# Batch 4's key-value product behind three pieces of group 2's first layer, and the r mix of group 2 ahead of its first square

## The chip, the cores and the metric

The kernel runs on one core of a Trainium2 chip. The metric is the device time of one execution in microseconds (us). The kernel before takes 201.94 us, the median of three runs from 201.52 to 202.92 us.

A core has engines that run beside each other, each with its own in-order queue of instructions: PE (TensorE, matrix products into PSUM), DVE (VectorE, elementwise work), ACT (ScalarE, activations, copies and scalings), POOL (GpSimd, here it only issues the large loads) and SP (SyncE, here it issues stores and small on-chip copies). Engines wait for each other through semaphores. An instruction that waits holds up everything behind it on its engine.

## The reference

Two layers follow each other. The first is a linear attention with an RMS norm per head, over 8 batches, 8 heads, 576 rows and 64 columns:

```
kv  = k^T v                       per batch and head, 64 x 64
out = q kv
out = out / sqrt(mean(out^2) + 1e-6) * g_norm
x   = the heads side by side      8 x 576 x 512
```

The second is a channel mix, in which each row is blended with the row before it of the same batch:

```
xk = mu_k * x + (1 - mu_k) * x_prev
xr = mu_r * x + (1 - mu_r) * x_prev
k  = relu(xk @ w_k)               512 -> 1024
v  = (k * k) @ w_v                1024 -> 512
r  = sigmoid(xr @ w_r)            512 -> 512
result = r * v
```

## The kernel before, in words

The attention goes by batches (0 to 7), each in two halves of four heads (z = 0 and 1). The channel mix goes by nine groups of 512 rows over all batches in one row; group 2 takes rows 1024 to 1535, so it needs the blended rows of batches 1 and 2.

The work is cut into pieces with names, and a hand-written string `ORDER` (L15) lists all of them in one sequence. `emit` (L41) walks through it and gives out the instructions of each piece to its engine. Each engine keeps the sequence in which the string names its own pieces. So moving a name in the string moves that piece in its engine's queue, against the other pieces of that engine alone. Waits are put in automatically, where an instruction reads or overwrites something that another engine handles. `@A` or `@D` behind a name chooses ACT or DVE.

The names that matter here, with B a batch and G a group:

- `ld.kB`, `ld.vB`, `ld.qB` (L226, L221): POOL issues the load of one batch of k, v or q, which is turned into bf16 on the way. The k and v buffers are a ring of three.
- `kvB.01` (L265): PE forms k^T v of batch B in 72 small products of 64x64. It needs that batch's k and v.
- `kcB` (L346, through `copy` at L128) copies the result out of PSUM, `ksB` (L271) sorts its even and odd rows with four products, `kdB` (L350, through `copy`) copies that out.
- `tqB` (L358): DVE transposes q. `uB` (L282): PE forms q kv in 16 products per half of the columns; it needs `kdB` and `tqB`.
- `sqB`, `ssB` (L388), `rsB` (L288): the squares, their sums per head, and one over the root, small and packed. `spB.z` (L430): SP spreads the small result over the partitions by four on-chip copies per half.
- `mulB.z` (L405), `dB.z` (L300), `mkB.z` and `mrB.z` (L136 on DVE, L134 on ACT), `xkB.z` and `xrB.z` (L313): the norm, the difference to the row before, its scaling by mu, and the blended rows for k and for r.
- `kG.F` (L507): four products, an eighth of group G's first layer. Two of them share one PSUM buffer, and then `reluG.H` (L465, ACT, H = F // 2) and `ksqG.H` (L522, DVE) make relu and its square from both.
- `rG.C` (L534) and `sigG.C2` (L544): the r product of 128 rows in four products, and the sigmoid of two of them. `vG.C.P` (L554): four products of the second layer. `outG.C2` (L567) and `stG.C` (L456): the product with the sigmoid on DVE, and the store by SP.

PSUM is a ring of four buffers (`ps`), taken in the order in which the string first uses them; whoever takes one waits until its last reader is done. Batch 2's `xk2.0` and `xk2.1` cover the two halves of the columns that the first layer sums over: of the four products of a piece `k2.F`, the first two read the half z = 0 and the last two read z = 1.

## Time and profile before

| | before |
|---|---|
| median of three runs | 201.94 us |
| the profiled execution, its own time | 201.43 us |
| its span (first to last instruction) | 199.6 us |
| PE busy | 190.3 us (95%) |
| DVE busy | 137.9 us (69%) |
| ACT busy | 122.0 us (61%) |
| POOL busy | 23.6 us (12%) |
| data moved by DMA | 30.63 MB |

The span is what the profile's time axis covers; the execution's own time has 1.83 us around it. The share of PE is an average over the whole span: where PE stands still is seen only in the time order of its instructions. In a timeline row the first number is the start, the second the length, both in us, then the engine, the line, the operation and the tiles (written <- read); the bracket tells how long the engine stood idle before it, and what ended that.

### The profile page before, as it was taken

What the parts mean: (1) busy time and instruction counts of PE and PEld (TensorE: products, weight loads), DVE (VectorE), ACT (ScalarE), POOL (GpSimd) and SP (SyncE); (2) the same over time, 40 slices, a digit from 0 to 9 for tenths busy, and PEclk for the clock granted to TensorE, in tenths of its full rate; (3) what the DMA queues carried; (4) which work ended last, traced back from release to release, by engine and by line L of the source; (5) the groups of instructions that cost most, each with busy time, mean ns of one, the idle gap of its engine ahead of it and who ended that gap; (6) DMA issues with size and microseconds to landing.
All of it is one profiled execution on the core that took longest, in us unless ns stands there. A gap on an engine that the chain in (4) does not pass through costs nothing.

```text
span 199.6 us, 4250 instructions
## 1 busy us (share of the span) xinstructions
PE 190.3 (95%) x1760; PEld 93.1 (47%) x1760; DVE 137.9 (69%) x235; ACT 122.0 (61%) x158; POOL 23.6 (12%) x42
## 2 busy tenths in 40 slices
PE   7899999999998799999999999999999999999992
PEld 2436854454443444444448744444444444444451
DVE  1669988897869396988968598799759421530741
ACT  3365599759967579945868986882319940423420
POOL 7734342041312010000000000000000000000000
PEclk9999999999999999999999999999999999999999
DMA  6999999999999999999402531643203000320344
GB/s 214 211 210 210 203 206 203 215 203 212 216 238 256 218 238 280 251 231 255 172 3 55 152 126 56 192 138 77 44 20 139 0 3 0 124 86 0 145 174 158
DMA packets 21031, 30.63 MB, mean 153 GB/s; under 512 B 1932, under 2 KB 14484, under 8 KB 21012
## 3 DMA queue, kind: packets, MB, share of 16 engines
q0 software_dynamic: 11280, 16.19, 45.3%
q1 hardware_dynamic: 9588, 14.03, 21.9%
q8 instruction: 14, 0.23, 0.4%
q10 hardware_dynamic: 144, 0.13, 0.2%
q14 instruction: 5, 0.04, 0.1%
HBM read 33.56 MB, written 9.44 MB: 215 GB/s over the span
## 4 chain that ended last, share of the span: by engine, by line
PE 76%; DMA 16%; ACT 2%; POOL 2%; issue 1%; DVE 1%; POOLq 0%; ACTq 0%
PE ps L554 28%; PE ps L507 24%; DMA k<-in_k_dram 16%; PE ps L534 13%; PE ps L482 3%; PE ps L265 3%; PE ps L282 2%; ACT relu L465 1%; PE ps L408 1%; PE ps L450 1%; PE ps L388 1%; PE ps L271 1%; POOL v L226 1%; POOL q L221 1%; ACT sq L379 1%
## 5 line engine op out<-in xcount | busy, mean ns | idle before, releaser
L554 PE MATMUL ps<-w_v,sqk 128*128 128x512 bf16 (+1 forms) x296 | 67.2, 374 | 0.0
L507 PE MATMUL ps<-xk,w_k 128*128 128x512 bf16 (+1 forms) x288 | 58.8, 356 | 0.5 <-issue 0.5
L465 ACT ACTIVATE relu<-ps 128x1024 bf16<-128x1024 f32 x36 | 36.5, 1025 | 35.1 <-PE ps L507 31.7
L554 PEld LDWEIGHTS <-sqk 128*128 128x128 bf16 x296 | 27.8, 98 | 32.2 <-issue 2.5
L507 PEld LDWEIGHTS <-w_k 128*128 128x128 bf16 x288 | 27.5, 98 | 26.9 <-issue 1.6
L567 DVE TENSOR_TENSOR out<-ps,sig 128x1024 f32<-128x1024 f32 x16 | 19.4, 1220 | 21.9 <-PE ps L554 12.5
L534 PE MATMUL ps<-w_r,xr 128*128 128x512 bf16 x144 | 34.0, 379 | 0.0
L522 DVE TENSOR_TENSOR sqk<-relu 128x1024 bf16<-128x1024 bf16 x32 | 21.2, 684 | 12.5 <-ACT relu L465 12.2
L544 ACT ACTIVATE sig<-ps 128x1024 bf16<-128x1024 f32 x18 | 18.2, 1024 | 12.4 <-PE ps L534 12.4
L534 PEld LDWEIGHTS <-xr 128*128 128x128 bf16 x144 | 13.8, 98 | 16.3 <-issue 0.5
L379 ACT ACTIVATE sq<-ps 128x576 bf16<-128x576 f32 x32 | 19.9, 652 | 1.8 <-PE ps L282 1.6
L144 ACT ACT_TABLE_LOAD x12 | 15.4, 1283 | 0.9 <-PEq L607 0.7
L358 DVE STREAM_TRANSPOSE qT<-q 128x576 f32<-128x576 f32 (+1 forms) x20 | 14.7, 760 | 1.8 <-DMA q<-in_q_dram 1.6
L136 DVE TENSOR_SCALAR uT<-ps,cols 128x576 bf16<-128x576 f32 x13 | 10.4, 816 | 6.9 <-ACT sq L379 4.8
L136 DVE TENSOR_SCALAR md<-d,cols 128x576 bf16<-128x576 bf16 x44 | 14.0, 370 | 0.4
L134 ACT ACTIVATE uT<-ps,cols 128x576 bf16<-128x576 f32 x15 | 10.9, 742 | 2.9 <-PE ps L282 2.9
L300 DVE TENSOR_TENSOR d<-xT 128x1152 bf16<-128x1152 bf16 (+1 forms) x18 | 12.3, 689 | 0.4
L313 DVE TENSOR_TENSOR xr<-md,xT 128x1152 bf16<-128x1152 bf16 x14 | 10.4, 751 | 1.6 <-ACT md L134 1.4
L405 DVE TENSOR_TENSOR xT<-uT,rs 128x1152 bf16<-128x1152 bf16 x14 | 10.4, 750 | 1.1 <-ACT rs L288 0.6
L313 DVE TENSOR_TENSOR xk<-md,xT 128x1152 bf16<-128x1152 bf16 x14 | 10.4, 754 | 0.6 <-ACT md L134 0.4
L450 PE MATMUL ps<-zero 128*128 128x512 bf16 x30 | 9.4, 454 | 1.2 <-DVE zero L164 1.2
L265 PE MATMUL ps<-v,k 64*64 64x64 bf16 x576 | 7.7, 194 | 2.4 <-DMA k<-in_k_dram 2.1
(53 smaller groups left out, 121.6 us busy)
## 6 DMA issues: line engine op xcount, KB each, us to landing
out_dram<-out SPq DMA_DIRECT2D x35, 256.0 KB, 2.3
v<-in_v_dram POOLq DMA_DIRECT2D x6, 576.0 KB, 22.6
k<-in_k_dram POOLq DMA_DIRECT2D x6, 576.0 KB, 23.1
q<-in_q_dram POOLq DMA_DIRECT2D x6, 576.0 KB, 23.9
rs<-rsc SPq DMA_DIRECT2D x48, 72.0 KB, 3.3
q<-in_q_dram POOLq DMA_DIRECT2D x4, 288.0 KB, 10.0
w_k<-in_moe_w_k_dram POOLq DMA_DIRECT2D x2, 512.0 KB, 11.0
w_v<-in_moe_w_v_dram POOLq DMA_DIRECT2D x2, 512.0 KB, 13.8
```

The costliest lines, as they stand in the source:

```text
L136: nc.vector.tensor_scalar(out=dst, in0=src, scalar1=col, scalar2=None, op0=ALU.mult)
L144: nc.scalar.preload_act_table_set(name)
L313: nc.vector.tensor_tensor(out=dst[:, 2 * z:2 * z + 2, r0:r0 + w], in0=md.t[:, :, cs], in1=xT[:, :, cur], op=ALU.add)
L358: nc.vector.transpose(out=dst[part, js], in_=src[part, js])
L379: sq_ = add("sq" + name, "A", lambda _, ps=ps, sq=sq, cs=cs, w=w: nc.scalar.activation(out=get(sq)[:, :, cs], in_=ps.t[:, :, 0:w], func=AF ...
L465: nc.scalar.activation(out=get(rt), in_=ps.t, func=AF.Relu)
L507: nc.tensor.matmul(get(ps)[:, fc % 2, a0:a1], w_k_sb[:, cc, 128 * fc:128 * fc + 128], xk[:, cc, x0:x0 + a1 - a0], start=(cc == 0), stop=(c ...
L522: nc.vector.tensor_mul(out=get(sqk)[:, 2 * f2:2 * f2 + 2, :], in0=rt.t, in1=rt.t)
L534: nc.tensor.matmul(get(ps)[:, ci % 2, :], xr[:, cc, n0:n0 + 128], w_r_sb[:, cc, :], start=(cc == 0), stop=(cc == NHP - 1))
L544: nc.scalar.activation(out=get(sg), in_=ps.t, func=AF.Sigmoid)
L554: nc.tensor.matmul(get(ps)[:, bank, cs], sqk.t[:, fc, 128 * ci:128 * ci + 128], w_v_sb[:, fc, cs], start=(fc == 0), stop=(fc == NFC - 1))
L567: dv = add(f"out{g}.{c2}", "D", lambda _, ps=ps, sg=sg, ot=ot: nc.vector.tensor_mul(out=get(ot), in0=ps.t, in1=sg.t), deps=ms + [sg_done], ...
```

## The change

Only the string `ORDER` differs, in one stretch. `kv4.01` stood right behind `v1.0.1`, ahead of the spreading of batch 2; it now stands behind `k2.2`, `k2.3` and `k2.0`. `kc4.01` follows it. In the DVE's sequence `ksq2.1` stood ahead of `xr2.0`, `mr2.1` and `xr2.1`; it now stands behind them.

```diff
 ... sq3.01 ss3 v1.0.1
-kv4.01
 sp2.0 sp2.1 rs3 st0.0 mul2.0 d2.0 mk2.0@D xk2.0 mul2.1 d2.1 mk2.1@D
 st0.1 sp3.0 mr2.0@A xk2.1 k2.2 sp3.1 out1.0 k2.3
-kc4.01@A
 out1.1 st1.3 k2.0
+kv4.01 kc4.01@A k2.1
 ks4.01 relu2.1 kd4.01@A st1.0
-ksq2.1 k2.1
-xr2.0 relu2.0 mr2.1@D xr2.1
+xr2.0 mr2.1@D xr2.1 ksq2.1 relu2.0
 tq4.01.0 tq4.01.1 ld.q7.01 k2.4 k2.5 relu2.2 k2.6 r2.2 r2.3 u4.01.0 ...
```

By engine: on PE the sequence was kv4, k2.2, k2.3, k2.0, ks4, k2.1, k2.4 and is now k2.2, k2.3, k2.0, kv4, k2.1, ks4, k2.4. On DVE it was out1.1, ksq2.1, xr2.0, mr2.1, xr2.1, tq4 and is now out1.1, xr2.0, mr2.1, xr2.1, ksq2.1, tq4. The sequences of ACT, POOL and SP are as they were.

More of the change, by code (lines that the diff above doesn't have):

```diff
@@ L15 @@
 ORDER = """
-ldh.k ldh.v seta setp perm ld.q0.0 ld.q0.1 ld.v0.1 ld.k0.1 ld.wk0 ident ld.wk1 ld.v1.1 ld.k1.1 ld.q1.1 ld.wr ld.q1.0 ld.v1.0 ld.k1.0 ld.wv0 ld.wv1 ld.v2.01 ld.k2.01 ld.q2.01 table small zz cst.k0@D cst.k1@A setb cst.v0@A cst.v1@D tq0.0.1 tq0.0.0 z:512 z:512 z:512 z:512 z:512 z:512 z:512 z:512 z:512 z:512 z:512 z:512 z:512 z:512 z:512 z:512 kv0.0 tq0.1.0 kc0.0@A z:512 z:512 ks0.0 tr9 cols kd0.0@A u0.0.0 sq0.00 z:512 z:512 z:512 ss0.00 u0.0.1 rs0.00 mul0.00 d0.00 tq0.1.1 z:512 z:512 kv0.1 ld.k3.01 ld.v3.01 ld.q3.01 sq0.01 kc0.1@A ss0.01 rs0.01 ks0.1 kd0.1@A z:512 z:512 z:512 u0.1.0 sq0.10 xk0.00 z:512 z:512 z:512 ss0.10 mul0.01 d0.01 xk0.01 rs0.10 mul0.10 d0.10 u0.1.1 k0.000 sq0.11 ss0.11 rs0.11 k0.110 xk0.10 k0.100 mul0.11 k0.001 d0.11 xk0.11 relu0.00 xr0.11 xr0.00 k0.010 k0.011 kv1.1 ksq0.00 k0.111 kc1.1@A tq1.1.0 tq1.1.1 ks1.1 xr0.10 relu0.01 kd1.1@A relu0.11 ksq0.11 k0.101 xr0.01 u1.1.1 uc1.11@A sq1.11 u1.1.0 sq1.10 uc1.10@D relu0.10 ksq0.10 r0.0 r0.1 ss1.2 ss1.3 rs1.2 rs1.3 mul1.1 kv1.0 ld.k5.01 ld.v5.01 kc1.0@D tq1.0.1 tq1.0.0 r0.2 r0.3 sig0.0 ks1.0 kd1.0@A ksq0.01 sig0.1 v0.0.0 u1.0.1 uc1.01@D u1.0.0 v0.1.0 sq1.00 sq1.01 uc1.00@D v0.1.1 d1.1 ss1.1 rs1.1 v0.0.1 out0.0 ss1.0 rs1.0 v0.2.0 v0.2.1 mul1.0 d1.0 mk1.0@D xk1.0 v0.3.0 v0.3.1 out0.1 mk1.1@A kv2.01 ld.v4.01 ld.k4.01 ld.q4.01 xk1.1 kc2.01@A mr1.1@A k1.0.0 k1.1.0 ks2.01 k1.2.0 k1.3.0 k1.2.1 kd2.01@A tq2.01.1 tq2.01.0 ld.q6.01 k1.3.1 relu1.1 k1.0.1 u2.01.1 sq2.11 mr1.0@D k1.1.1 uc2.01@D k1.6.0 k1.7.0 k1.6.1 relu1.0 uc2.11@D u2.01.0 sq2.01 sq2.10 sq2.00 uc2.10@D k1.7.1 k1.4.0 k1.5.0 xr1.1 k1.4.1 uc2.00@A ss2 kv3.01 ld.k7.01 ld.v7.01 xr1.0 rs2 ksq1.0 kc3.01@D relu1.3 tq3.01.0 tq3.01.1 ld.q5.01 k1.5.1 relu1.2 ksq1.3 r1.0 ks3.01 kd3.01@A r1.2 ksq1.1 ksq1.2 r1.1 sig1.0 r1.3 sig1.1 u3.01.0 sq3.00 v1.2.0 uc3.00@D v1.3.0 v1.2.1 sq3.10 u3.01.1 uc3.11@A uc3.10@D kv5.01 ld.k6.01 ld.v6.01 sq3.11 kc5.01@A v1.3.1 v1.1.0 ks5.01 kd5.01@A v1.1.1 uc3.01@A v1.0.0 sq3.01 ss3 v1.0.1 kv4.01 sp2.0 sp2.1 rs3 st0.0 mul2.0 d2.0 mk2.0@D xk2.0 mul2.1 d2.1 mk2.1@D st0.1 sp3.0 mr2.0@A xk2.1 k2.2 sp3.1 out1.0 k2.3 kc4.01@A out1.1 st1.3 k2.0 ks4.01 relu2.1 kd4.01@A st1.0 ksq2.1 k2.1 xr2.0 relu2.0 mr2.1@D xr2.1 tq4.01.0 tq4.01.1 ld.q7.01 k2.4 k2.5 relu2.2 k2.6 r2.2 r2.3 u4.01.0 sig2.1 sq4.00 k2.7 ksq2.0 relu2.3 ksq2.2 v2.1.0 v2.0.0 uc4.10@A uc4.00@D u4.01.1 ksq2.3 v2.1.1 mul3.0 uc4.01@A st1.1 tq6.01.0 d3.0 sq4.10 mk3.0@D uc4.11@A v2.0.1 r2.0 sq4.11 r2.1 sq4.01 ss4 st0.3 v2.3.0 rs4 v2.3.1 sig2.0 st1.2 mul3.1 d3.1 mr3.1@D v2.2.0 v2.2.1 mk3.1@D xk3.0 xk3.1 sp4.1 sp4.0 xr3.1 out2.0 k3.6 st2.1 k3.7 mr3.0@D xr3.0 k3.4 relu3.3 ksq3.3 out2.1 tq5.01.0 tq5.01.1 st2.2 mul4.1 k3.5 relu3.2 ksq3.2 k3.2 k3.3 relu3.1 ksq3.1 r3.0 k3.0 k3.1 relu3.0 ksq3.0 r3.1 d4.1 sig3.0 mk4.1@D r3.2 r3.3 xk4.1 tq6.01.1 sig3.1 v3.2.0 u5.01.1 uc5.01@A v3.2.1 uc5.11@A mul4.0 d4.0 v3.0.0 mr4.1@D v3.3.0 sq5.01 sq5.11 u5.01.0 uc5.00@A mk4.0@D sq5.00 sq5.10 v3.1.0 uc5.10@A v3.1.1 st0.2 v3.0.1 mr4.0@D kv6.01 out3.0 kc6.01@A st2.3 xk4.0 xr4.0 ss5 rs5 sp5.0 v3.3.1 out3.1 ks6.01 st3.1 k4.6 kd6.01@A k4.7 relu4.3 u6.01.0 uc6.00@A uc6.10@D sp5.1 tq7.01.0 sq6.00 k4.2 xr4.1 k4.3 sq6.10 relu4.1 k4.0 k4.1 relu4.0 r4.2 ksq4.3 r4.3 ksq4.0 st3.0 tq7.01.1 ksq4.1 k4.4 k4.5 u6.01.1 uc6.01@D sig4.1 relu4.2 ksq4.2 st3.3 r4.0 v4.1.0 sq6.11 r4.1 uc6.11@A sig4.0 v4.1.1 st3.2 mul5.1 mul5.0 d5.1 sq6.01 v4.3.0 mk5.1@D d5.0 v4.0.0 v4.0.1 kv7.01 mr5.1@A ss6 v4.2.0 mk5.0@D xk5.0 xk5.1 kc7.01@A ks7.01 out4.0 kd7.01@D st4.0 v4.2.1 xr5.1 rs6 sp6.1 u7.01.1 uc7.01@A uc7.11@A v4.3.1 sq7.11 out4.1 st4.3 st2.0 st4.2 sq7.01 k5.2 k5.3 relu5.1 mr5.0@D xr5.0 ksq5.1 u7.01.0 sq7.10 uc7.10@D sp6.0 uc7.00@D k5.0 k5.1 relu5.0 ksq5.0 mul6.1 k5.4 d6.1 mk6.1@D sq7.00 st4.1 k5.6 k5.7 relu5.3 ksq5.3 k5.5 relu5.2 ksq5.2 mul6.0 d6.0 ss7 rs7 v5.1.0 v5.2.0 v5.2.1 r5.2 v5.3.0 mk6.0@D mr6.1@D xk6.0 xr6.1 mr6.0@D r5.0 xr6.0 r5.1 sig5.0 r5.3 sig5.1 xk6.1 v5.0.0 sp7.1 v5.0.1 mul7.1 v5.3.1 out5.1 r6.0 r6.1 k6.4 sp7.0 k6.5 mul7.0 v5.1.1 out5.0 st5.0 k6.6 k6.7 relu6.3 relu6.2 k6.2 k6.3 d7.1 mk7.1@A d7.0 mr7.0@D mk7.0@D xk7.0 sig6.0 relu6.1 st5.3 st5.2 r6.2 r6.3 sig6.1 mr7.1@A k6.0 xk7.1 xr7.0 k6.1 k8.4 k7.2 ksq6.2 k7.3 k8.0 k8.1 relu7.1 k7.0 ksq6.3 xr7.1 k7.1 ksq6.1 relu6.0 relu8.0 k8.2 k8.3 k8.5 ksq6.0 v6.0.0 v6.0.1 v6.1.0 ksq7.1 relu7.0 ksq7.0 relu8.2 v6.2.0 v6.3.0 v6.2.1 v6.3.1 k7.6 out6.1 st6.2 k7.7 v6.1.1 relu7.3 st6.3 ksq7.3 out6.0 k7.4 k7.5 k8.6 v7.2.0 relu7.2 ksq7.2 v7.0.0 v7.2.1 relu8.1 v7.0.1 r7.0 r7.1 st6.0 ksq8.1 v7.3.0 sig7.0 v7.1.0 ksq8.0 st5.1 r7.2 r7.3 v7.3.1 sig7.1 v7.1.1 out7.0 v8.1.00 out7.1 st7.2 k8.7 relu8.3 ksq8.3 st7.3 st6.1 r8.0 st7.1 r8.1 r8.2 r8.3 ksq8.2 v8.0.00 v8.1.10 sig8.0 st7.0 v8.2.00 v8.2.10 out8.10 st8.10 sig8.1 out8.20 st8.20 v8.0.10 out8.00 v8.3.00 v8.3.10 out8.30 st8.00 st8.30 v8.3.01 v8.3.11 out8.31 st8.31
@@ new lines @@
+ldh.k ldh.v seta setp perm ld.q0.0 ld.q0.1 ld.v0.1 ld.k0.1 ld.wk0 ident ld.wk1 ld.v1.1 ld.k1.1 ld.q1.1 ld.wr ld.q1.0 ld.v1.0 ld.k1.0 ld.wv0 ld.wv1 ld.v2.01 ld.k2.01 ld.q2.01 table small zz cst.k0@D cst.k1@A setb cst.v0@A cst.v1@D tq0.0.1 tq0.0.0 z:512 z:512 z:512 z:512 z:512 z:512 z:512 z:512 z:512 z:512 z:512 z:512 z:512 z:512 z:512 z:512 kv0.0 tq0.1.0 kc0.0@A z:512 z:512 ks0.0 tr9 cols kd0.0@A u0.0.0 sq0.00 z:512 z:512 z:512 ss0.00 u0.0.1 rs0.00 mul0.00 d0.00 tq0.1.1 z:512 z:512 kv0.1 ld.k3.01 ld.v3.01 ld.q3.01 sq0.01 kc0.1@A ss0.01 rs0.01 ks0.1 kd0.1@A z:512 z:512 z:512 u0.1.0 sq0.10 xk0.00 z:512 z:512 z:512 ss0.10 mul0.01 d0.01 xk0.01 rs0.10 mul0.10 d0.10 u0.1.1 k0.000 sq0.11 ss0.11 rs0.11 k0.110 xk0.10 k0.100 mul0.11 k0.001 d0.11 xk0.11 relu0.00 xr0.11 xr0.00 k0.010 k0.011 kv1.1 ksq0.00 k0.111 kc1.1@A tq1.1.0 tq1.1.1 ks1.1 xr0.10 relu0.01 kd1.1@A relu0.11 ksq0.11 k0.101 xr0.01 u1.1.1 uc1.11@A sq1.11 u1.1.0 sq1.10 uc1.10@D relu0.10 ksq0.10 r0.0 r0.1 ss1.2 ss1.3 rs1.2 rs1.3 mul1.1 kv1.0 ld.k5.01 ld.v5.01 kc1.0@D tq1.0.1 tq1.0.0 r0.2 r0.3 sig0.0 ks1.0 kd1.0@A ksq0.01 sig0.1 v0.0.0 u1.0.1 uc1.01@D u1.0.0 v0.1.0 sq1.00 sq1.01 uc1.00@D v0.1.1 d1.1 ss1.1 rs1.1 v0.0.1 out0.0 ss1.0 rs1.0 v0.2.0 v0.2.1 mul1.0 d1.0 mk1.0@D xk1.0 v0.3.0 v0.3.1 out0.1 mk1.1@A kv2.01 ld.v4.01 ld.k4.01 ld.q4.01 xk1.1 kc2.01@A mr1.1@A k1.0.0 k1.1.0 ks2.01 k1.2.0 k1.3.0 k1.2.1 kd2.01@A tq2.01.1 tq2.01.0 ld.q6.01 k1.3.1 relu1.1 k1.0.1 u2.01.1 sq2.11 mr1.0@D k1.1.1 uc2.01@D k1.6.0 k1.7.0 k1.6.1 relu1.0 uc2.11@D u2.01.0 sq2.01 sq2.10 sq2.00 uc2.10@D k1.7.1 k1.4.0 k1.5.0 xr1.1 k1.4.1 uc2.00@A ss2 kv3.01 ld.k7.01 ld.v7.01 xr1.0 rs2 ksq1.0 kc3.01@D relu1.3 tq3.01.0 tq3.01.1 ld.q5.01 k1.5.1 relu1.2 ksq1.3 r1.0 ks3.01 kd3.01@A r1.2 ksq1.1 ksq1.2 r1.1 sig1.0 r1.3 sig1.1 u3.01.0 sq3.00 v1.2.0 uc3.00@D v1.3.0 v1.2.1 sq3.10 u3.01.1 uc3.11@A uc3.10@D kv5.01 ld.k6.01 ld.v6.01 sq3.11 kc5.01@A v1.3.1 v1.1.0 ks5.01 kd5.01@A v1.1.1 uc3.01@A v1.0.0 sq3.01 ss3 v1.0.1 sp2.0 sp2.1 rs3 st0.0 mul2.0 d2.0 mk2.0@D xk2.0 mul2.1 d2.1 mk2.1@D st0.1 sp3.0 mr2.0@A xk2.1 k2.2 sp3.1 out1.0 k2.3 out1.1 st1.3 k2.0 kv4.01 kc4.01@A k2.1 ks4.01 relu2.1 kd4.01@A st1.0 xr2.0 mr2.1@D xr2.1 ksq2.1 relu2.0 tq4.01.0 tq4.01.1 ld.q7.01 k2.4 k2.5 relu2.2 k2.6 r2.2 r2.3 u4.01.0 sig2.1 sq4.00 k2.7 ksq2.0 relu2.3 ksq2.2 v2.1.0 v2.0.0 uc4.10@A uc4.00@D u4.01.1 ksq2.3 v2.1.1 mul3.0 uc4.01@A st1.1 tq6.01.0 d3.0 sq4.10 mk3.0@D uc4.11@A v2.0.1 r2.0 sq4.11 r2.1 sq4.01 ss4 st0.3 v2.3.0 rs4 v2.3.1 sig2.0 st1.2 mul3.1 d3.1 mr3.1@D v2.2.0 v2.2.1 mk3.1@D xk3.0 xk3.1 sp4.1 sp4.0 xr3.1 out2.0 k3.6 st2.1 k3.7 mr3.0@D xr3.0 k3.4 relu3.3 ksq3.3 out2.1 tq5.01.0 tq5.01.1 st2.2 mul4.1 k3.5 relu3.2 ksq3.2 k3.2 k3.3 relu3.1 ksq3.1 r3.0 k3.0 k3.1 relu3.0 ksq3.0 r3.1 d4.1 sig3.0 mk4.1@D r3.2 r3.3 xk4.1 tq6.01.1 sig3.1 v3.2.0 u5.01.1 uc5.01@A v3.2.1 uc5.11@A mul4.0 d4.0 v3.0.0 mr4.1@D v3.3.0 sq5.01 sq5.11 u5.01.0 uc5.00@A mk4.0@D sq5.00 sq5.10 v3.1.0 uc5.10@A v3.1.1 st0.2 v3.0.1 mr4.0@D kv6.01 out3.0 kc6.01@A st2.3 xk4.0 xr4.0 ss5 rs5 sp5.0 v3.3.1 out3.1 ks6.01 st3.1 k4.6 kd6.01@A k4.7 relu4.3 u6.01.0 uc6.00@A uc6.10@D sp5.1 tq7.01.0 sq6.00 k4.2 xr4.1 k4.3 sq6.10 relu4.1 k4.0 k4.1 relu4.0 r4.2 ksq4.3 r4.3 ksq4.0 st3.0 tq7.01.1 ksq4.1 k4.4 k4.5 u6.01.1 uc6.01@D sig4.1 relu4.2 ksq4.2 st3.3 r4.0 v4.1.0 sq6.11 r4.1 uc6.11@A sig4.0 v4.1.1 st3.2 mul5.1 mul5.0 d5.1 sq6.01 v4.3.0 mk5.1@D d5.0 v4.0.0 v4.0.1 kv7.01 mr5.1@A ss6 v4.2.0 mk5.0@D xk5.0 xk5.1 kc7.01@A ks7.01 out4.0 kd7.01@D st4.0 v4.2.1 xr5.1 rs6 sp6.1 u7.01.1 uc7.01@A uc7.11@A v4.3.1 sq7.11 out4.1 st4.3 st2.0 st4.2 sq7.01 k5.2 k5.3 relu5.1 mr5.0@D xr5.0 ksq5.1 u7.01.0 sq7.10 uc7.10@D sp6.0 uc7.00@D k5.0 k5.1 relu5.0 ksq5.0 mul6.1 k5.4 d6.1 mk6.1@D sq7.00 st4.1 k5.6 k5.7 relu5.3 ksq5.3 k5.5 relu5.2 ksq5.2 mul6.0 d6.0 ss7 rs7 v5.1.0 v5.2.0 v5.2.1 r5.2 v5.3.0 mk6.0@D mr6.1@D xk6.0 xr6.1 mr6.0@D r5.0 xr6.0 r5.1 sig5.0 r5.3 sig5.1 xk6.1 v5.0.0 sp7.1 v5.0.1 mul7.1 v5.3.1 out5.1 r6.0 r6.1 k6.4 sp7.0 k6.5 mul7.0 v5.1.1 out5.0 st5.0 k6.6 k6.7 relu6.3 relu6.2 k6.2 k6.3 d7.1 mk7.1@A d7.0 mr7.0@D mk7.0@D xk7.0 sig6.0 relu6.1 st5.3 st5.2 r6.2 r6.3 sig6.1 mr7.1@A k6.0 xk7.1 xr7.0 k6.1 k8.4 k7.2 ksq6.2 k7.3 k8.0 k8.1 relu7.1 k7.0 ksq6.3 xr7.1 k7.1 ksq6.1 relu6.0 relu8.0 k8.2 k8.3 k8.5 ksq6.0 v6.0.0 v6.0.1 v6.1.0 ksq7.1 relu7.0 ksq7.0 relu8.2 v6.2.0 v6.3.0 v6.2.1 v6.3.1 k7.6 out6.1 st6.2 k7.7 v6.1.1 relu7.3 st6.3 ksq7.3 out6.0 k7.4 k7.5 k8.6 v7.2.0 relu7.2 ksq7.2 v7.0.0 v7.2.1 relu8.1 v7.0.1 r7.0 r7.1 st6.0 ksq8.1 v7.3.0 sig7.0 v7.1.0 ksq8.0 st5.1 r7.2 r7.3 v7.3.1 sig7.1 v7.1.1 out7.0 v8.1.00 out7.1 st7.2 k8.7 relu8.3 ksq8.3 st7.3 st6.1 r8.0 st7.1 r8.1 r8.2 r8.3 ksq8.2 v8.0.00 v8.1.10 sig8.0 st7.0 v8.2.00 v8.2.10 out8.10 st8.10 sig8.1 out8.20 st8.20 v8.0.10 out8.00 v8.3.00 v8.3.10 out8.30 st8.00 st8.30 v8.3.01 v8.3.11 out8.31 st8.31
```

## The prediction

> **What bounds the kernel now.** I read the page first, then the chain of waits, then the time order of PE around its one long gap.
>
> The page's head and the first lines of its chain:
>
> ```profile
> span 199.6 us, 4250 instructions
> ...
> PE 190.3 (95%) x1760; PEld 93.1 (47%) x1760; DVE 137.9 (69%) x235; ACT 122.0 (61%) x158; POOL 23.6 (12%) x42
> ...
> PE 76%; DMA 16%; ACT 2%; POOL 2%; issue 1%; DVE 1%; POOLq 0%; ACTq 0%
> ```
>
> PE holds most of the chain, but 16% of it is one kind of transfer. The chain in order of time says which one (start, length, what), and a table by stretches shows PE there and after it (length; busy time and count of PE, PEld, DVE, ACT and POOL; granted clock; DMA share; GB/s):
>
> ```profile
> 41.99 23.98 DMA k<-in_k_dram
> 65.97 0.04 issue
> 66.02 0.78 PE ps L265 x72
> 66.79 2.70 PE ps L507 x12
> 69.49 0.22 PE ps L271 x4
> 69.71 3.45 PE ps L507 x16
> 73.17 1.73 PE ps L534 x8
> ...
> 103.21 0.71 PE ps L265 x72
> ```
>
> ```profile
> 64.20:66.10 1.90, 0.16 (x9) 0.09 (x12) 1.90 (x3) 1.90 (x3) 0.00 (x0) 1.00 1.14 221
> ...
> 66.00:196.00 130.00, 129.69 (x988) 62.08 (x988) 85.59 (x138) 75.72 (x92) 0.54 (x1) 1.00 0.46 123
> ```
>
> The chain runs through the load of batch 4's k, which lands at 41.99 + 23.98 = 65.97 us, and `kv4` starts 0.05 us later. From there on PE works 129.69 of 130.00 us. So everything behind 66 us is set by how much PE has left to do, and the last stall that can move the end is the one ahead of `kv4`. What stands at PE, DVE and ACT around it, from the timeline:
>
> ```profile
> 63.23 1.04 PE L554 MATMUL ps<-w_v,sqk 128*128 128x512 bf16 x4
> 66.02 0.78 PE L265 MATMUL ps<-v,k 64*64 64x64 bf16 x72 [1.74 <-DMA k<-in_k_dram]
> ...
> 63.73 0.76 DVE L313 TENSOR_TENSOR xk<-md,xT 128x1152 bf16<-128x1152 bf16 x1
> 64.40 2.35 DVE L567 TENSOR_TENSOR out<-ps,sig 128x1024 f32<-128x1024 f32 x2
> 69.78 0.69 DVE L522 TENSOR_TENSOR sqk<-relu 128x1024 bf16<-128x1024 bf16 x1 [3.03 <-ACT relu L465]
> 70.39 0.75 DVE L313 TENSOR_TENSOR xr<-md,xT 128x1152 bf16<-128x1152 bf16 x1
> 71.06 0.64 DVE L136 TENSOR_SCALAR md<-d,cols 128x576 bf16<-128x576 bf16 x2
> 71.73 0.76 DVE L313 TENSOR_TENSOR xr<-md,xT 128x1152 bf16<-128x1152 bf16 x1
> 72.41 1.43 DVE L358 STREAM_TRANSPOSE qT<-q 128x576 f32<-128x576 f32 x2
> ...
> 64.76 1.43 ACT L134 ACTIVATE md<-d,cols 128x576 bf16<-128x576 bf16 x2
> 66.86 0.37 ACT L128 CAST kvn<-ps 128x256 bf16<-128x256 f32 x1 [0.67 <-PE ps L265]
> 68.72 1.02 ACT L465 ACTIVATE relu<-ps 128x1024 bf16<-128x1024 f32 x1 [1.49 <-PE ps L507]
> 73.38 1.28 ACT L144 ACT_TABLE_LOAD   x1
> 74.93 1.02 ACT L544 ACTIVATE sig<-ps 128x1024 bf16<-128x1024 f32 x1 [0.27 <-PE ps L534]
> ```
>
> `v1.0.1` ends at 63.23 + 1.04 = 64.27, and PE then stands 1.74 us for a load, while `xk2.1`, the last input of group 2's first layer, is ready at 63.73 + 0.76 = 64.49.
>
> **The change part by part.**
>
> *kv4 behind k2.2, k2.3, k2.0.* PE work is neither added nor removed: 72 small products and their weight loads change places with 12 large ones. What goes is the cover. Before, from 64.27 to the end of the two r pieces, PE takes 1.75 (wait) + 0.78 + 2.70 + 0.22 + 3.45 + 1.73 = 10.63 us, which is 74.90. After: 16 large products in a row take 3.45, so twelve that follow `v1.0.1` without a switch take 12/16 of it, 2.59 us; `kv4` without a wait takes 0.71, as batch 6's does at 103.21; `k2.1` behind a switch to small products takes 4/16 of 3.45 and the 0.11 that the twelve at 66.79 took over their 2.59, so 0.97; `ks4` 0.22; `k2.4` to `k2.6` 2.59; the two r pieces 1.73. Sum 8.81 us, to 73.08. The difference is 1.82 us.
>
> Can the cover start at once? The first two products of `k2.2` read the half z = 0, ready long before; the third reads `xk2.1`. Two products are 0.43 us, so it is wanted near 64.7 by the modelled ends or 64.5 by starts (63.23 + six products of 0.216), against 64.49. That is a wait between 0 and 0.2 us; I take 0.1. Does it last? Three pieces end at 64.27 + 2.59 = 66.86, and the load lands at 65.97: 0.89 us to spare. The gain is 1.82 - 0.1, about **1.7 us**. If the cover is gone, each us of it costs one.
>
> *Buffers.* `k2.2`, `k2.0` and `kv4` now take the three PSUM buffers that `kv4`, `k2.2` and `k2.0` took, in this order; `kv4` gets the one that `out1.0` frees, the first of the two at 64.40, so at about 65.6: earlier than 66.86, no cost. `k2.6` takes the buffer of `k2.2` instead of `kv4`'s, so it waits for `relu2.1`, and its first weight load also waits for PE's own `k2.3`, eight products and a `kv4` earlier. The `r2.2` piece waits for `relu2.0`.
>
> *ACT, same sequence.* `kc4` waits for `kv4` (67.57) and stands ahead of `relu2.1`, `kd4`, `relu2.0`, `relu2.2`. By 0.37 and 1.02: `kc4` to 68.0, `relu2.1` to 69.0, `kd4` (behind `ks4`, 68.76; I take 0.37 for it, as for `kc4`, the same size) to 69.4, `relu2.0` to 70.5, `relu2.2` (PE's `k2.5` ends 70.5) to 71.5, the table load to 72.8. PE wants `relu2.1` at `k2.6` (70.5), `relu2.0` at `r2.2` (71.35), `kd4` at `u4` (73.08): 1.5, 0.9 and 3.7 us to spare. The sigmoid needs the table at 73.1: 0.3 to spare, as now (73.38 + 1.28 against 74.93). Nothing lost.
>
> *xr2.0, mr2.1, xr2.1 ahead of ksq2.1.* DVE stands 3.03 us idle before `ksq2.1`, and `mr2.0` on ACT is done at 64.76 + 1.43 = 66.19, so the three fit there: from 66.75 by 0.67 steps (70.39 to 71.06 to 71.73) to about 68.9. `ksq2.1` follows `relu2.1`, to 69.8, `tq4` to 71.2. Without this part the sequence would be `ksq2.1` to 69.8, `xr2.1` to 71.9, `tq4` to 73.3: the r pieces, now at 71.35 to 73.08, want `xr2.1` at their third product (71.8) and `u4` wants `tq4` at 73.08. So this part saves no time by itself, and guards 0.1 to 0.3 us that the first would lose. `tq4` also needs batch 4's q, issued at 43.2, with
>
> ```profile
> L221 POOL DMA_DIRECT2D q<-in_q_dram x1: 543/543/543, 43.2 to 43.2; - x1
> ...
> DMA to landing us min/median/max: 25.6/25.6/25.6
> ```
>
> so at 68.8, 1.0 us before it is wanted. The one DMA that moves is `ld.q7`, which POOL issues behind `tq4`, some 2 us earlier; all other large loads of the ring are already queued ahead of it. SP's sequence and its stores are untouched.
>
> *Sum.* The profiled execution took 201.43 us; 201.43 - 1.7 = 199.7. The median of the three runs is 0.51 above it; from there 200.2. I take **200.0**, since part of the 0.51 may be the same load landing later, which the new order covers up to 0.89 us further. From no change, a measurement of this kernel can tell about 1% (2 us).
>
> **The rivals.**
>
> *Larger, because the load is later than in the profile.* Up to 2.59 us of waiting can be covered. For: all three runs took longer than the profiled one, and DMA is at a share of 1.14 in the gap. If the whole 0.51 is this load, the wait is 2.25 and the result 201.94 - 2.2 = 199.7; at the full cover 199.3. Against: nothing shows where the 0.51 lies.
>
> *Given back at the spreading of batch 4.* [...] `mul4.1` waits for its four on-chip copies, of which the last was issued at 85.3:
>
> ```profile
> DMA to landing us min/median/max: 5.2/5.9/6.5
> ...
> 91.91 0.76 DVE L405 TENSOR_TENSOR xT<-uT,rs 128x1152 bf16<-128x1152 bf16 x1
> 92.58 1.28 DVE L522 TENSOR_TENSOR sqk<-relu 128x1024 bf16<-128x1024 bf16 x2
> 94.69 0.69 DVE L522 TENSOR_TENSOR sqk<-relu 128x1024 bf16<-128x1024 bf16 x1 [0.83 <-ACT relu L465]
> ...
> rs<-rsc SPq DMA_DIRECT2D x48, 72.0 KB, 3.3
> ```
>
> It lands at 91.8 and `mul4.1` starts at 91.91, on the edge. All 48 such copies have a median of 3.3 us, these up to 6.5, so they are slowed by loads. If the landing stays at 91.8 while all else comes 1.7 us earlier, the squares of group 3 behind it stay too. DVE's 0.83 us of idle time there takes up half; the other 0.9 would reach PE: 200.0 + 0.9 = 200.9, or 201.7 if a second place like it takes the rest. Against: if latency stays 6.5 us, it moves with its issue.
> [...]
>
> *Slower: the new head of PE's queue waits for batch 2's spreading.* `kv4` no longer fills the time until `xk2.1`. Its DVE work starts at the landing of the copies for `mul2.0`:
>
> ```profile
> L430 SPq DMA_DIRECT2D rs<-rsc x3: 585/592/594, 50.7 to 51.9; - x3
> ...
> DMA to landing us min/median/max: 6.2/6.2/6.3
> ...
> 58.27 0.76 DVE L405 TENSOR_TENSOR xT<-uT,rs 128x1152 bf16<-128x1152 bf16 x1 [0.42 <-DVE uT L136]
> ```
>
> The fourth copy, issued at 51.9, lands at 58.1, and from 58.27 DVE works without a pause to `xk2.1`. If it lands later by d, `k2.2` stops for d less the 0.2. The gain is gone from d of about 2.0, and at 2.7, where the old order would begin to wait too, the new one is 0.75 us slower: 201.94 + 0.75 = 202.7. For: no slack on DVE there. Against: it needs 8.2 us instead of the 6.2 to 6.5 shown.
>
> *The change does not do what it says.* Other waits keep `k2.2` back, and the gap stays: 201.9. For it speaks only that a buffer's last reader may be one that I placed wrongly; the buffers above were free.
>
> **How the numbers follow.** Forecast 50%, split about one third below the 1% bound (199.9) and two thirds above it, since it spans 199.7 to 200.2. Larger gain 27%, faster by over 1%. Given back 14%, within 1%. New wait in front 4%, within 1% at 202.7. No effect 2%; a rest of 3% for something slower that no row shows. So faster 0.44 (0.17 + 0.27), same 0.53, slower 0.03. The range goes from 199.2, just under the full cover, to 201.3, inside the given-back case (200.9 to 201.7); what lies outside is the tail of that case, the last three cases, and spread.
>
> **What would show it.** Right: `k2.2` starts near 64.2, no wait over 0.2 us at its third product; `kv4` near 66.9 with no wait for k; the r pieces end near 73.1 with no wait for `xr2.1`; `u4` starts near 73.0 instead of 74.82; DVE's idle time of 3.03 us is below 1; PE stays without a gap to the end, and the span is about 197.9. Wrong: a wait for k still in front of `kv4`; a wait at `k2.2` for `xk2.1`; an idle time of DVE ahead of `mul4.1` with PE waiting at group 3's second layer; or the same 1.7 us earlier at 90 us but not at the end.

## The result, and the profile after

| | before | after |
|---|---|---|
| median | 202.43 us (six runs, 201.42 to 203.66) | 199.94 us (six runs, 199.44 to 200.35) |
| the profiled execution, its own time | 201.43 us | 200.13 us |
| its span | 199.6 us | 198.4 us |

The ratio is 0.9874 with a 95% interval of 0.9827 to 0.9920: faster by a little over 1%. Before's six runs lie in two groups, 201.42 to 201.94 and 202.92 to 203.66, which makes its median of this set high (over all sets 19 of its 77 runs are above 202.5 us, none of 12 of the new order, and no profile caught one); in three later sets of 32, 22 and 17 runs it was 201.57, 201.66 and 201.77 us. So the change is worth 1.6 to 1.8 us by those, and 2.5 us by the first set.

The page after, its head and the first line of its chain:

```profile
span 198.4 us, 4225 instructions
...
PE 188.4 (95%) x1735; PEld 93.3 (47%) x1760; DVE 137.8 (69%) x235; ACT 121.8 (61%) x158; POOL 23.7 (12%) x42
...
PE 68%; DMA 26%; POOL 2%; issue 2%; DVE 0%; POOLq 0%
```

The share of PE is the same 95%. 25 of its 1760 products have no record here, and where one is missing the views show a pause of 0.05 or 0.16 us that is not there. The chain's share of DMA has grown, but by transfers that end ahead of the change, the last of them batch 5's v, for `kv5`. The stretch around the change, by engine (start, length, what):

```profile
63.74 1.04 PE L554 MATMUL ps<-w_v,sqk 128*128 128x512 bf16 x4
64.61 2.75 PE L507 MATMUL ps<-xk,w_k 128*128 128x512 bf16 x12
67.29 0.78 PE L265 MATMUL ps<-v,k 64*64 64x64 bf16 x72
...
71.69 1.89 PE L534 MATMUL ps<-w_r,xr 128*128 128x512 bf16 x8
73.51 0.45 PE L282 MATMUL ps<-qT,kv 32*64 32x288 bf16 x16
...
64.09 0.76 DVE L313 TENSOR_TENSOR xk<-md,xT 128x1152 bf16<-128x1152 bf16 x1
67.08 0.75 DVE L313 TENSOR_TENSOR xr<-md,xT 128x1152 bf16<-128x1152 bf16 x1
69.62 0.69 DVE L522 TENSOR_TENSOR sqk<-relu 128x1024 bf16<-128x1024 bf16 x1 [0.44 <-ACT relu L465]
90.50 0.76 DVE L405 TENSOR_TENSOR xT<-uT,rs 128x1152 bf16<-128x1152 bf16 x1
```

`k2.2` to `k2.0` follow `v1.0.1` without a pause, `kv4` follows them without a wait for its load, and DVE's idle time of 3.03 us has shrunk to 0.44. The same stretch over PE, as the table by stretches has it:

```profile
64.30:66.10 1.80, 1.80 (x10) 0.78 (x8) 1.80 (x3) 1.79 (x4) 0.05 (x1) 1.00 1.16 221
```

PE is busy for all 1.80 us, where before it was busy for 0.16 of 1.90.

Two distances say where the time went. The rows of before behind its wait, and then the chain's last step, of before and of after:

```profile
66.72 2.77 PE L507 MATMUL ps<-xk,w_k 128*128 128x512 bf16 x12
...
73.00 1.89 PE L534 MATMUL ps<-w_r,xr 128*128 128x512 bf16 x8
74.82 0.45 PE L282 MATMUL ps<-qT,kv 32*64 32x288 bf16 x16
```

```profile
195.74 0.42 DVE out L581
```

```profile
194.43 0.42 DVE out L581
```

From `v1.0.1`'s start to `u4`'s, before takes 74.82 - 63.23 = 11.59 us and after 73.51 - 63.74 = 9.77: 1.82 us less. From `u4` to the last step, before takes 195.74 - 74.82 = 120.92 us and after 194.43 - 73.51 = 120.92: nothing is given back. The remaining difference lies ahead of the change: after reached `v1.0.1` 0.51 us later, in code that is the same in both. That is scatter: over the profiles below `v1.0.1` starts between 62.96 and 63.80 us in the old order and between 63.24 and 63.74 in the new (kv5_late aside, which moves more). So the two spans differ by 1.2 us only.

### The profile page after: what moved, and what is told of

Same layout as the page of the kernel before. It is cut to its first block, busy times and chain, and to the rows that moved or that the text cites. A ratio compares the mean times of both kernels' runs of the same rounds, so it can differ in the third digit from the quotient of the medians.

```text
span 198.4 us, 4225 instructions
## 1 busy us (share of the span) xinstructions
PE 188.4 (95%) x1735; PEld 93.3 (47%) x1760; DVE 137.8 (69%) x235; ACT 121.8 (61%) x158; POOL 23.7 (12%) x42
## 4 chain that ended last, share of the span: by engine, by line
PE 68%; DMA 26%; POOL 2%; issue 2%; DVE 0%; POOLq 0%
PE ps L554 27%; PE ps L507 24%; DMA v<-in_v_dram 19%; PE ps L534 12%; DMA w_v<-in_moe_w_v_dram 7%; PE ps L282 2%; PE ps L265 1%; PE ps L388 1%; POOL w_k L252 1%; POOL q L221 1%; PE ps L271 0%; POOL k L226 0%; POOL perm L189 0%; POOL v L226 0%; DVE out L581 0%
## 5 line engine op out<-in xcount | busy, mean ns | idle before, releaser
L554 PE MATMUL ps<-w_v,sqk 128*128 128x512 bf16 (+1 forms) x286 | 65.7, 373 | 0.9 <-issue 0.6
L507 PE MATMUL ps<-xk,w_k 128*128 128x512 bf16 (+1 forms) x280 | 58.1, 355 | 1.1 <-issue 0.8
L282 PE MATMUL ps<-qT,kv 32*64 32x288 bf16 x256 | 8.5, 290 | 0.8 <-DVE qT L358 0.8
```

The lines of the kernel that those rows point to most:

```text
L507: nc.tensor.matmul(get(ps)[:, fc % 2, a0:a1], w_k_sb[:, cc, 128 * fc:128 * fc + 128], xk[:, cc, x0:x0 + a1 - a0], start=(cc == 0), stop=(c ...
L554: nc.tensor.matmul(get(ps)[:, bank, cs], sqk.t[:, fc, 128 * ci:128 * ci + 128], w_v_sb[:, fc, cs], start=(fc == 0), stop=(fc == NFC - 1))
```

## The experiments

Theory A: all of the gain is PE's wait for batch 4's k, as far as the pieces ahead of `kv4` cover it; the DVE part guards it. Theory B: the sequence itself, or the earlier r mix, carries it. Theory C: the landing differs between executions and the gain with it. D and E are named where they come up. The table has the two distances for every profile, worked out as above, and then times and ratios to before with their intervals.

| run | `v1.0.1` to `u4` | `u4` to end | median | ratio |
|---|---|---|---|---|
| before | 11.59 | 120.92 | 201.57 to 202.43 | 1 |
| before_look | 11.55 | 120.92 | 201.29 (one run) | |
| after | 9.77 | 120.92 | 199.94 | 0.9874 [0.9827, 0.9920] |
| whole_again | 10.21 | 120.92 | 200.12 | 0.9883 [0.9838, 0.9928] |
| kv_only | 10.33 | 120.92 | 200.28 | 0.9926 [0.9892, 0.9959] |
| xr_only | 11.10 | 120.92 | 201.53 | 1.0002 [0.9971, 1.0032] |
| behind_one | 10.97 | 120.92 | 200.71 | 0.9945 [0.9924, 0.9965] |
| behind_four | 10.23 | 121.08 | 199.95 | 0.9916 [0.9890, 0.9941] |
| before_half | 10.35 | 120.92 | 200.17 | 0.9928 [0.9896, 0.9960] |
| after_half | 9.97 | 120.93 | 199.55 | 0.9898 [0.9864, 0.9931] |
| before_extra | 15.29 | 120.93 | 204.35 | 1.0119 [1.0078, 1.0160] |
| after_extra | 10.57 | 120.92 | 200.42 | 0.9931 [0.9904, 0.9958] |
| kv5_late | 12.15 | 120.93 | 201.07 | 0.9938 [0.9907, 0.9969] |

The third column is the same to 0.01 us in all but one: whatever is gained or lost up to `u4` reaches the end. (kv5_late's second column holds `kv5`'s 0.7 us and `ks5`'s 0.2 too.)

### Each part alone

kv_only, against after:

```diff
-xr2.0 mr2.1@D xr2.1 ksq2.1 relu2.0
+ksq2.1 xr2.0 mr2.1@D xr2.1 relu2.0
```

> Only kv4 and kc4 are moved; on DVE the first square of group 2 keeps its place ahead of the r mix. Theory A (all of the gain is the wait for batch 4's k that three pieces cover, and the DVE part only guards it): PE has no wait in front of kv4, but r2.2 or u4 waits 0.1 to 0.3 us for DVE, and the time is 0.1 to 0.3 us above the whole change's 199.94 us, so 200.0 to 200.3. Theory B (the earlier r mix carries the gain): close to the kernel before, 201.5 to 202.5 us.

xr_only, against before:

```diff
-ksq2.1 k2.1 xr2.0 relu2.0 mr2.1@D xr2.1
+k2.1 xr2.0 mr2.1@D xr2.1 ksq2.1 relu2.0
```

> Only the r mix is put ahead of the first square; kv4 stays in front of the k product. Theory A: DVE's 3.0 us of idle time is filled, PE still waits 1.7 us or more for batch 4's k in front of kv4, and the time is that of the kernel before within 0.5%. Theory B: 1 to 2.5 us faster than before.

The timeline of kv_only, PE and then DVE:

```profile
64.97 2.32 PE L507 MATMUL ps<-xk,w_k 128*128 128x512 bf16 x10 [0.15 <-DVE xk L313]
...
71.73 2.02 PE L534 MATMUL ps<-w_r,xr 128*128 128x512 bf16 x8
...
71.46 0.76 DVE L313 TENSOR_TENSOR xr<-md,xT 128x1152 bf16<-128x1152 bf16 x1
```

and of xr_only:

```profile
66.09 0.78 PE L265 MATMUL ps<-v,k 64*64 64x64 bf16 x72 [1.25 <-DMA k<-in_k_dram]
...
69.85 0.69 DVE L522 TENSOR_TENSOR sqk<-relu 128x1024 bf16<-128x1024 bf16 x1 [0.27 <-ACT relu L465]
```

The kv part alone is 200.28 us. Its eight r products take 2.02 us instead of 1.89, since `xr2.1` is done at 72.22 and they begin at 71.73: the 0.13 us that the guard is for. The r mix alone gives nothing (1.0002), though it cuts DVE's idle time from 3.03 to 0.27 us; PE still waits for k. Theory B in its second form (the earlier r mix carries the gain) falls.

### How much cover

behind_one, against after:

```diff
-xk2.1 k2.2 sp3.1 out1.0 k2.3 out1.1 st1.3 k2.0 kv4.01 kc4.01@A k2.1
+xk2.1 k2.2 kv4.01 sp3.1 out1.0 k2.3 out1.1 st1.3 k2.0 kc4.01@A k2.1
```

> kv4 stands behind k2.2 alone, so 0.86 us of work covers the wait instead of 2.59; the rest is as in the whole change. Theory A: in the profile PE waits at kv4 until its k lands, 0.5 to 1.0 us for a landing near 66 us, and the gain over before is 0.86 us plus at most 0.1, so a ratio near 0.996. If the landing differs between executions (theory C), the time spreads as before's runs do (2 us), where the whole change's runs spread 0.9 us. If any place behind the first piece did as well (theory D: only the head of the queue mattered), the ratio is that of the whole change, 0.987.

behind_four, against after:

```diff
-k2.0 kv4.01 kc4.01@A k2.1 ks4.01 relu2.1 kd4.01@A st1.0
+k2.0 k2.1 kv4.01 kc4.01@A relu2.1 st1.0
 ...
-tq4.01.0 tq4.01.1 ld.q7.01 k2.4 k2.5
+tq4.01.0 tq4.01.1 ld.q7.01 k2.4 ks4.01 kd4.01@A k2.5
```

> kv4 stands behind four pieces, 3.45 us of cover; ks4 and kd4 move back by one piece too. Theory A with the landing of the profile: nothing left to cover, so the whole change's 199.9 us within 0.3, perhaps 0.2 slower since relu2.1 on ACT stands behind kc4 and comes 0.9 us later. Theory C (in some executions the load lands later than three pieces cover): faster by up to 0.5 us, with less spread than 0.9 us.

PE's timeline in behind_one, and in behind_four:

```profile
64.11 1.03 PE L507 MATMUL ps<-xk,w_k 128*128 128x512 bf16 x4
66.27 0.78 PE L265 MATMUL ps<-v,k 64*64 64x64 bf16 x72 [1.13 <-DMA k<-in_k_dram]
```

```profile
65.22 3.18 PE L507 MATMUL ps<-xk,w_k 128*128 128x512 bf16 x14 [0.29 <-DVE xk L313]
68.33 0.78 PE L265 MATMUL ps<-v,k 64*64 64x64 bf16 x72
```

One piece gains 201.57 - 200.71 = 0.86 us by the medians, the length of the piece, and leaves a wait of 1.13. That the two agree so well is partly chance: in the profile the gain is 11.59 - 10.97 = 0.62, because `kv4` starts at 66.27 there instead of 66.02. Either way the gain follows the cover, so theory D (only the head of the queue matters) falls. A fourth piece adds nothing (199.95 against 199.94 and 200.12): with three there was no wait left, in the profile or, as far as the medians show, outside it. That speaks against theory C, as does behind_one: PE still waits for the load there, and its 12 runs spread 0.69 us, not 2.

### The landing itself, earlier and later

before_half and after_half, in the function that issues the loads, with the old order and with the new:

```diff
             m = slice(2 * zs[0], 2 * zs[-1] + 2)
+            if n == "v" and b == 4:
+                m = slice(0, 2)
             nc.gpsimd.dma_start(out=get(kvq[(n, b)])[:, m, :], in_=view[:, m, :])
+            if n == "k" and b == 4:
+                nc.gpsimd.memset(get(kvq[("v", b)])[:, 2:4, :], 0.0)
```

> The old order, with half of batch 4's v left out of its load (the other half is filled with zeros by POOL), so that the load of k behind it lands about half a load's spacing earlier, 1.7 us (v lands near 62.6 and k at 65.97). The result is not the reference's for the heads of batch 4 that are left out. Theory A (the wait for k in front of kv4 is what the change removes): kv4 starts near 64.3 with no wait or a few tenths, and the old order becomes as fast as the new one, 1.4 to 1.8 us faster than before. Theory B (the gain lies in the sequence itself): the time of before.

> The new order with the same half left out. Theory A: the load was covered already, so nothing changes: the time of the whole change, within 0.3 us. Theory B: 1.4 to 1.8 us faster than before_half. If this is faster than the whole change by 0.3 us or more, another wait for a load (kv5's v, 0.35 us) counts too.

before_extra and after_extra, likewise:

```diff
             nc.gpsimd.dma_start(out=get(kvq[(n, b)])[:, m, :], in_=view[:, m, :])
+            if n == "v" and b == 4:
+                nc.gpsimd.dma_start(out=extra, in_=view[:, 0:2, :])
```

> The old order with an extra load of half a tensor, into a tile that nobody reads, between batch 4's v and k, so that k lands about 1.7 us later. Theory A: PE's wait in front of kv4 grows from 1.7 to about 3.4 us and the time by 1.7 us, a ratio near 1.008 to before.

> The new order with the same extra load. Theory A: three pieces cover 2.59 us; of the 1.7 us later landing 0.4 to 0.9 us are covered, and a wait of 0.8 to 1.3 us for k appears in front of kv4, so the time is 0.8 to 1.3 us above the whole change's, and 2.4 to 2.6 us below before_extra's. Theory E (the load's landing sets the end in both orders): the same distance of 1.7 us to before_extra as between the two orders without the extra load.

`kv4` and what follows it on PE in before_half; in before_extra, with two stretches of its table; and in after_extra:

```profile
64.55 0.78 PE L269 MATMUL ps<-v,k 64*64 64x64 bf16 x72 [0.50 <-DMA k<-in_k_dram]
```

```profile
67.81 0.79 PE L268 MATMUL ps<-v,k 64*64 64x64 bf16 x72 [3.81 <-DMA k<-in_k_dram]
68.53 4.39 PE L510 MATMUL ps<-xk,w_k 128*128 128x512 bf16 x12
...
64.00:67.80 3.80, 0.00 (x1) 0.00 (x0) 2.92 (x3) 1.92 (x3) 0.74 (x1) 1.00 1.17 215
67.80:72.00 4.20, 4.19 (x81) 1.96 (x82) 0.00 (x0) 0.37 (x1) 0.00 (x0) 0.59 1.06 225
```

```profile
67.95 0.78 PE L268 MATMUL ps<-v,k 64*64 64x64 bf16 x72 [0.73 <-DMA k<-in_k_dram]
```

With the load 1.5 us earlier (`kv4` at 64.55 instead of 66.02) the old order is at 200.17 us, almost where the new one is, without any change of sequence; the new order moves from 199.94 and 200.12 to 199.55, inside the intervals of each other. This is the difference that theory A asks for: the same edit is worth 1.5 us to the old order and at most 0.6 to the new one. Theory B in its first form (the sequence itself carries the gain) falls too: it asked for the time of before. The new order did move by more than the 0.3 that I had allowed, 0.39 and 0.57. I had named `kv5`'s wait for its v as a reason for that; it is 0.35 us in after and gone in after_half, but in whole_again it is gone as well, so this stays open.

With the load 1.8 us later, the new order waits 0.73 us, a little less than the 0.8 to 1.3 expected, and loses 0.3 to 0.5 us by the medians. The old one waits 3.81 us, 2.07 more than before, and its end comes at 199.18 us, 3.44 later. The part that I had not expected is in the second row: the twelve products behind the wait take 4.39 us instead of 2.77, at a mean granted clock of 0.59. So its ratio is 1.0119 where 1.008 was expected. Theory E (the landing sets the end in both orders alike) falls: the two orders are 3.9 us apart here. Theory A had 2.4 to 2.6; the 1.6 us of the slower products were in none of the expectations.

### Again, and a further step

> The kernel before once more with a profile, to see how far the landing of batch 4's k and PE's wait for it differ between executions: theory C (they differ, and so does the gain): a wait off 1.74 us by 0.5 us or more, and a time that differs from 201.43 us by the same amount. Against it: the same wait within 0.2 us.

> The whole change once more, on the chip of this set. Theory A: 199.6 to 200.3 us and a ratio of 0.989 to 0.993 to before; no wait for k in front of kv4, and the third product of k2.2 at the edge of its wait for xk2.1 (0 to 0.3 us).

PE in before_look, then PE, DVE and POOL in whole_again:

```profile
65.87 0.78 PE L265 MATMUL ps<-v,k 64*64 64x64 bf16 x72 [1.71 <-DMA k<-in_k_dram]
```

```profile
64.26 3.03 PE L507 MATMUL ps<-xk,w_k 128*128 128x512 bf16 x12
...
63.20 0.93 DVE L136 TENSOR_SCALAR md<-d,cols 128x576 bf16<-128x576 bf16 x2
63.28 0.74 POOL L226 DMA_DIRECT2D v<-in_v_dram  x1 [2.90 <-DMA v<-in_v_dram]
```

The old order's wait is 1.71 us, 0.03 off the first, and its time of 201.29 us is 0.14 off. In three profiles of the old order's place for `kv4` (before, before_look, xr_only) it starts at 66.02, 65.87 and 66.09. Theory C finds no support in the executions that were profiled: the landing hardly moves, and the wait of 1.25 us in xr_only is shorter because PE came later.

The whole change again is 200.12 us. Its twelve first-layer products take 3.03 us instead of 2.75, so 0.28 us go into the wait for `xk2.1` at the third product. Another 0.15 of its 10.21 against 9.77 lie in `kv4`, which takes 0.93 instead of 0.78; no row gives a reason.

kv5_late, against after, puts `kv5` in front of that place, to fill it and to be rid of `kv5`'s own wait for its v:

```diff
-kv5.01 ld.k6.01 ld.v6.01 sq3.11 kc5.01@A v1.3.1 v1.1.0 ks5.01 kd5.01@A v1.1.1
+sq3.11 v1.3.1 v1.1.0 v1.1.1
 ...
-ss3 v1.0.1 sp2.0 sp2.1 rs3
+ss3 v1.0.1 kv5.01 ld.k6.01 ld.v6.01 sp2.0 sp2.1 rs3 kc5.01@A
 ...
-k2.2 sp3.1 out1.0 k2.3
+k2.2 sp3.1 ks5.01 kd5.01@A out1.0 k2.3
```

> The whole change, and in addition kv5 moves from behind u3 (where it waits 0.35 us for batch 5's v) to right behind v1.0.1, in front of k2.2, with kc5 behind rs3 and ks5, kd5 behind k2.2. Theory A: the 0.35 us wait goes, and kv5's 0.71 us lies in front of k2.2's wait for xk2.1, so that goes too: 0.3 to 0.6 us faster than the whole change, 199.3 to 199.6 us. Rival: the buffers of batch 5's k and v come free 5.8 us later and the loads of batch 6 are issued later; if the queue of loads runs dry, kv6 waits and the time is above the whole change's.

```profile
64.52 0.59 PE L507 MATMUL ps<-xk,w_k 128*128 128x512 bf16 x2 [0.23 <-DVE xk L313]
...
67.70 0.39 PE L507 MATMUL ps<-xk,w_k 128*128 128x512 bf16 x1
68.89 0.81 PE L507 MATMUL ps<-xk,w_k 128*128 128x512 bf16 x3 [0.79 <-issue]
```

It is slower than the whole change, 201.07 us instead of the 199.3 to 199.6 expected. The wait for v is gone, the one for `xk2.1` is still 0.23 (PE came earlier), and a new pause of 0.79 us stands inside `k2.1`, behind its first product. "issue" means that the profile knows of nothing that it waited for. The rival expected (loads running dry) is not it: behind 66 us this pause is the only idle time of PE. It comes after two blocks of 72 small products within 5 us; what it is stays open, as no run here tests it.

## Why the prediction was right, point by point

**The time.** 200.0 was forecast, 199.94 and 200.12 us were measured. The way there holds in its main term and less well in its base. The sum of 1.82 us for the cover, 1.7 with the new wait, was measured as 1.82 in the first profile (11.59 to 9.77) and 1.38 in the second (10.21), and as 1.6 to 1.8 by the medians. From 201.43 the forecast would have been 199.7; I raised that to 200.0 by the 0.51 us up to the median of three runs, and said that part of it might be the same load. The runs show no such part: the old order's `kv4` starts within 0.22 us in three profiles. The raise came out right in size, as the later medians are 201.57 to 201.77, but not for that reason, and that 200.0 lies about 0.1 us from both results is luck. What makes the runs above 202.5 us is in none of the profiles and stays open; before_half, whose wait for k is only 0.50 us, has runs 1.4 and 1.9 us above its median too, so it is not shown to be that wait.

**The signs.** No wait for k in front of `kv4`, none for `xr2.1` at the r pieces, and 0.44 us of idle time on DVE came as named. `u4` (73.51 and 73.60) and the span (198.4) came 0.5 us later than named: in after because `v1.0.1` did, in whole_again half by the wait for `xk2.1`, which I had listed as a sign of being wrong.

**The wait at `k2.2`.** I took 0.1, between 0 and 0.2. Measured, as the time by which the products of the pieces ahead of `kv4` took longer than without a wait: none in after, behind_one and after_extra, 0.21 in after_half, 0.28 in whole_again, 0.32 in kv_only, 0.45 in behind_four. The brackets of 0.15 (kv_only) and 0.29 (behind_four) in the rows above are smaller, since the two products before the gap are drawn with 0.59 us there instead of the 0.43 that two such products take in a row. So the mechanism is right, and both the 0.1 and the bound of 0.2 were too low. The rival built on it (a late spreading) needed 2.0 us to take the gain away and came nowhere near, but in small it is there, as the next point shows.

**Why it differs.** Two things make `xk2.1` late against PE. One is where its chain of DVE work starts: `mul2.0` starts 4.96 us ahead of `v1.0.1` in before, 4.89 in after, 4.73 in whole_again, 4.64 in kv_only, 4.53 in behind_four and 4.52 in after_half. In after_half this acts alone: d is 0.44 against before, and the prediction's "d less the 0.2" gives 0.24 for the 0.21 measured. The other, which I left out, is the scaling `mk2.1` just ahead of `xk2.1`. Its two instructions take 0.65 us in after and after_half, 0.88 in kv_only, 0.92 in behind_four and 0.93 in whole_again. In each of the four runs the two delays against after add up to the wait plus 0.16 to 0.18, which is what after had to spare.

The scaling's length goes with an issue on POOL. In whole_again, POOL issues the load of batch 6's v from 0.08 us behind its start; in after POOL begins later, 0.13 behind it:

```profile
63.40 0.65 DVE L136 TENSOR_SCALAR md<-d,cols 128x576 bf16<-128x576 bf16 x2
63.53 0.82 POOL L226 DMA_DIRECT2D v<-in_v_dram  x1 [2.80 <-DMA v<-in_v_dram]
```

In after it is POOL's issue that is longer, 0.82 instead of 0.74. Over the profiles: where POOL's issue started up to 0.25 us ahead of the pair or in its first 0.1 us, the pair took 0.79 to 0.93 (before, before_look, whole_again, kv_only, behind_four, before_extra); where POOL came later or elsewhere, 0.65 (the other seven). The rows show the two lengths together, 0.14 to 0.28 us more on DVE and, in after, 0.08 more on POOL; what joins them they do not show. In kv_only, where POOL starts 0.24 us ahead of the pair, its two instructions take 0.61 and 0.35 us; in before, 0.06 ahead, 0.50 and 0.37; in after 0.37 both, though POOL starts while the first one runs. No run here moved POOL's issue on purpose, so that this issue makes the scaling longer is a guess from a pattern, not shown.

**The DVE part.** "It saves no time by itself, and guards 0.1 to 0.3 us": xr_only 1.0002, and kv_only 0.13 us at the r products, as placed. Right.

**Buffers and ACT.** No wait for a PSUM buffer or for ACT shows in after's stretch; the sigmoid follows the r products by the same 0.27 us as before:

```profile
73.61 1.02 ACT L544 ACTIVATE sig<-ps 128x1024 bf16<-128x1024 f32 x1 [0.27 <-PE ps L534]
```

Right.

**The rivals.** *Larger*: its mechanism did not show in any profile; a fourth piece of cover gained nothing. *Given back at the spreading of batch 4*: `mul4.1` moved from 91.91 to 90.50 without idle time, 120.92 us from `u4` to the end in both. The landing moved with its issue, as the copies of `sp4.1` in after show:

```profile
L430 SPq DMA_DIRECT2D rs<-rsc x2: 592/592/593, 83.4 to 84.0; - x2
...
DMA to landing us min/median/max: 5.2/5.8/6.5
```

The last, issued at 84.0, lands at 90.5, after the same 6.5 us as in before (85.3 to 91.8). The 0.9 us of this rival needs a landing that stays at 91.8, and no run shows one; what sets the 6.5 us is not shown either. The rows show them beside the loads: in before the DMA share is 1.18 from 85.3 to 91.8, and copies issued from 124.4 to 130.8, where the queue of the loads moved nothing, land after 2.0 to 2.3 us.

*The change does not do what it says*: excluded by the rows above.

**The chances.** 0.53 stood on "within 1%" and 0.44 on faster by more. The ratios of 0.9874 and 0.9883 lie just past that bound, and both intervals hold it (0.9920 and 0.9928): a gain of 1.6 to 1.8 us is 0.8 to 0.9% of 201.6, and the rest comes from before's runs above 202.5 us.

## What to carry to other kernels

Where PE is busy everywhere else, as here (129.69 of 130.00 us behind the wait), its wait for a load is worth about its length (1.74 us; 1.38 and 1.82 in two profiles), and it is removed by putting work that is ready in front of the waiting piece: in these runs the gain followed the smaller of the wait and of that work, 0.6 (by the profile) to 0.9 us (by the medians) for one piece of 0.86 us, 1.4 to 1.8 for three of 2.59, no more for four. When such a piece moves up, everything that it will read must be followed up to its own last input; the guard on DVE was worth 0.13 us, and the new edge (`xk2.1`) cost 0 to 0.45. Two distances, up to the end of the changed stretch and from there to the last instruction, tell at once whether anything is given back.

## What the runs showed of the hardware

In before_extra PE's wait for k is 3.81 us, where before has 1.74, and the end comes 3.44 us later for 2.07 us more of waiting: the granted clock was 1.00 behind the wait of before (66.00 to 196.00) and a mean of 0.59 over the 4.2 us behind that of before_extra (1.00 again from 72.00 to 76.00), and twelve products took 4.39 us instead of 2.77, 1.6 us on top of the wait. The new order with the same later load waits 0.73 us, and its profiled execution has a mean granted clock of 1.00. In these profiles a wait of 1.74 us went without such a loss and one of 3.81 with it; from which length on it comes, and whether the wait is its cause, no run here shows.

One profile has a lower clock without a long wait. In xr_only it falls early in the kernel:

```profile
0.00:10.00 10.00, 7.51 (x68) 3.58 (x69) 4.17 (x19) 3.36 (x5) 7.27 (x19) 1.00 0.85 207
10.00:15.00 5.00, 4.98 (x64) 2.30 (x59) 3.48 (x8) 2.68 (x5) 1.94 (x3) 0.66 1.15 205
```

Within the span PE had stood idle for at most 1.2 us at a time before it, and the run's time of 201.48 us is not above the others. What set it off is not shown, so a wait that stays short is no promise of a clock of 1.00.
